# A causal mask as a matrix product, finer waits and finer pacing in a two-branch attention kernel

## The chip, the cores and the metric

The kernel runs on one core of one Trainium2 chip. The metric is the device time of one execution in microseconds (us). One core has five engines that each work through their own instruction list in order: TensorE (PE, matrix products; its weight loads are a row of their own, PEld), VectorE (DVE), ScalarE (ACT), GpSimd (POOL) and SyncE (SP, which issues transfers). Engines wait for one another only through semaphores.

## What is computed

Two attention branches over the same 2048 x 576 input are mixed by a sigmoid gate. Branch A is recurrent: 64 segments of 32 tokens, each with 8 memory tokens that are an output of the segment before.

```python
def _A_ref(x, mem0, Wq, Wk, Wv, Wo, seg_len):
    ...
    mask = (idx[:, None] < M) | (idx[:, None] >= idx[None, :])
    mem = mem0
    for s in range(n_seg):
        xs = x[:, s * seg_len:(s + 1) * seg_len, :].copy()
        h = jnp.concatenate([mem, xs], axis=1)
        ...
        scores = jnp.where(mask[None, None], scores, -1000000000.0)
        p = _softmax(scores, axis=-1)
        o = jnp.einsum('bhqk,bhke->bhqe', p, v)
        o = jnp.einsum('bhte,hed->btd', o, Wo)
        mem = o[:, :M, :].copy()
        outs.append(o[:, M:, :])
    return jnp.concatenate(outs, axis=1)

def _B_ref(x, wqkv, wo):
    ...
    p = _softmax(scores, axis=-1)
    o = jnp.einsum('bhqk,bhkd->bhqd', p, v)
    ...
g = _sigmoid((x * gate_w).sum(-1, keepdims=True))
return g * a + (1 - g) * b
```

Branch A has 32 heads of 128, 40 positions in a segment (8 + 32) and a 40 x 40 softmax, here called the small softmax. Branch B is an ordinary softmax attention with 32 heads of 18 over 2048 x 2048 scores.

## The kernel before

**A planner writes the order.** The program does not issue instructions where the Python code stands. Each piece of work is recorded with `add` (L132): engine or engines that may do it, an estimated duration, the pieces it depends on, a priority, and the buffers ("tokens") that it takes and gives back. `Plan.run` (L151) and `Plan.choose` (L251) then place the pieces on the five engines one after the other, and this fixes the instruction order of every engine. The priorities and thresholds come from the table `RANKS` (L17), one row for each 16 segments. The duration estimates are used for the order alone: on the chip every engine runs its list as fast as the semaphores let it. When the planner foresees a gap on PE of more than about 0.3 us, it puts in a filler (L829): a group of four products with a zero matrix, added to an accumulator that is open anyway (`warm`, L182).

**Branch B** is cut into 512 visits (L842 on). A visit is a group of four score products on PE (`sb`, L858), one exponential of 128 x 2048 on ACT (`etb`, L867), and a group of four value products on PE (`ob`, L876). The scores of a visit fill four of the eight PSUM banks and there is one such buffer, so the next score group waits for the exponential. Every 16 visits an output is normalised by four VectorE operations (L904 to L919) and stored by POOL.

**Branch A, one segment.** `ht` (the 8 memory tokens and 24 of the 32 new ones, transposed) is multiplied into six pieces of Q, K and V (`pvv`, L1201, 30 groups of four products), which are copied out of PSUM (`tm`), and Q and K are transposed by DMA (`tt`, L1293) and put in place by VectorE (`qk`, L1302). The heads come in two halves. For each half: 32 score products (`psh`, L1325) into one PSUM bank; an exponential on ACT (`et`, L1335); a minimum with the constant `cap` on DVE (L1341), which is 3e38 where the mask allows and 0 where it forbids; the row sums as 12 small products (`pss`, L1356); a reciprocal on DVE (L1368); its spread over the rows as 12 products (`prb`, L1382); a multiplication on DVE (L1393); 16 products with V (`pso`, L1404); two copies to `ot` (L1414, recorded through the helper lines L472 on ACT and L474 on DVE). The output product (`out_pieces`, L1099; 128 products on L1109 in eight pieces of 16, four to a half) starts for each half when both copies of that half are there. Then `ob_cast` (L1436) copies the result `acc` to `obf`, `ob_bd` (L1439) reads `acc` again in PSUM and multiplies its last 16 columns with a mask into `bd`, the fold (`pw`, L1461, 12 small products) turns the memory rows round, and L1471 writes them into the `ht` of the next segment. This loop from `ht` to `ht` is serial over 64 segments.

The last 8 tokens of every segment don't feed the memory: their projections are computed outside the loop in `la` units (`last_unit`, L955, lines L946 and L950), two for each of most segments, and their output product is `lo` (L1490), once per four segments.

**What ties the branches.** The gate list at the end (L1657 to L1663) gives a visit a dependency on a piece of branch A: the first `ahead` visits are free, the last `behind` come after, and the others are dealt over the 64 segments. Before, all visits of a segment depend on one piece, the first projection (`seg_gate[s] = uq0`, L1233).

Of the kernel before, what the change touches and what calls it, by code (L numbers as in the profile page):

```python
# [10 lines left out]
BF16 = mybir.dt.bfloat16  # L11
# [7 lines left out]
        "switch": 0.101, "near": 0, "early": 1.104, "wait": 0.393, "Q0": 2.363, "K0": 2.711, "Q1": 4.67,  # L19
        "K1": 3.397, "V0": 5.924, "V1": 5.379, "t0": 0.94, "t1": 0.398, "ph0": 9.657, "ph1": 0.05, "sm0": 1.041,  # L20
        "sm1": 2.745, "bc0": 0.781, "bc1": 0.697, "po0": 0.142, "po1": 0.573, "op0": 3.391, "op1": 0.536,
        "fo": 2.847, "lo0": 7.697, "lo1": 1.76, "la": 2.503, "ob": 1.356, "eQ": 5.996, "eK": 4.139, "eV": 3.462,
        "co": 11.428, "le": 6.917, "xp": 4.684, "mn": 1.531, "ct": 3.999, "fin": 17.485, "la_gate": 1,
        "lo_gate": 1, "ahead": 53, "behind": 12, "tail": 0.25, "qc": 5.203, "gap": 0.082, "cool": 863.098,
        "tp": 0.05, "cp": 0.05,
    },
    {
        "switch": 0.566, "near": 0, "early": 0.879, "wait": 0.574, "Q0": 2.035, "K0": 2.767, "Q1": 5.001,
        "K1": 3.913, "V0": 5.813, "V1": 5.624, "t0": 2.693, "t1": 3.024, "ph0": 10.481, "ph1": 0.05, "sm0": 1.356,
        "sm1": 2.806, "bc0": 0.705, "bc1": 1.374, "po0": 0.16, "po1": 0.85, "op0": 4.548, "op1": 0.05,  # L30
        "fo": 2.442, "lo0": 6.471, "lo1": 1.6, "la": 2.902, "ob": 1.514, "eQ": 4.303, "eK": 1.887, "eV": 2.757,
        "co": 9.646, "le": 7.257, "xp": 4.622, "mn": 1.072, "ct": 2.98, "fin": 18.697, "la_gate": 1, "lo_gate": 1,
        "ahead": 53, "behind": 12, "tail": 0.25, "qc": 4.212, "gap": 0.025, "cool": 604.648, "tp": 0.059,
        "cp": 2.5,
    },
    {
        "switch": 0.933, "near": 0.062, "early": 0.442, "wait": 0.458, "Q0": 3.101, "K0": 3.266, "Q1": 4.507,
        "K1": 3.879, "V0": 5.715, "V1": 5.233, "t0": 1.746, "t1": 1.52, "ph0": 8.719, "ph1": 0.544, "sm0": 0.98,
        "sm1": 2.636, "bc0": 0.878, "bc1": 1.593, "po0": 0.05, "po1": 0.666, "op0": 4.211, "op1": 0.142,
        "fo": 1.753, "lo0": 7.609, "lo1": 3.613, "la": 2.285, "ob": 0.938, "eQ": 3.915, "eK": 1.776, "eV": 4.854,  # L40
        "co": 10.047, "le": 4.881, "xp": 4.775, "mn": 0.059, "ct": 3.249, "fin": 19.989, "la_gate": 1,
        "lo_gate": 1, "ahead": 53, "behind": 12, "tail": 0.399, "qc": 4.172, "gap": 0.021, "cool": 833.588,
        "tp": 1.502, "cp": 2.715,
    },
    {
        "switch": 0.842, "near": 0.056, "early": 0.478, "wait": 0.257, "Q0": 0.05, "K0": 3.207, "Q1": 4.114,
        "K1": 3.963, "V0": 4.848, "V1": 4.944, "t0": 1.753, "t1": 1.675, "ph0": 9.689, "ph1": 0.593, "sm0": 2.541,
        "sm1": 2.776, "bc0": 2.467, "bc1": 1.373, "po0": 2.298, "po1": 0.768, "op0": 7.231, "op1": 0.203,
        "fo": 1.659, "lo0": 7.93, "lo1": 3.297, "la": 0.05, "ob": 1.161, "eQ": 3.254, "eK": 0.05, "eV": 6.854,
        "co": 9.595, "le": 4.095, "xp": 3.302, "mn": 0.33, "ct": 2.917, "fin": 18.443, "la_gate": 1, "lo_gate": 1,  # L50
        "ahead": 53, "behind": 12, "tail": 0.332, "qc": 5.346, "gap": 0.021, "cool": 6051.615, "tp": 2.782,
        "cp": 4.189,
# [23 lines left out]
class Plan:  # L76
# [74 lines left out]
    def run(self):  # L151
# [18 lines left out]
        while len(order) < n + extra:  # L170
# [54 lines left out]
            dirty |= set(free)  # L225
# [7 lines left out]
            for t in op.take:  # L233
                held = self.tokens[t]
                got = max(x for x in held if x[0] <= est + 1e-9)
                held.remove(got)
                op.slots.setdefault(t, []).append(got[1])
                dirty |= set(free)
            for t, taker, k in op.give:
                self.tokens[t].append((op.end + op.tail + self.DRAIN[pick], taker.slots[t][k]))  # L240
                dirty |= set(free)
# [70 lines left out]
def kernel(  # L312
# [68 lines left out]
    cap = const.tile([P, L], BF16, name="cap")  # L381
# [7 lines left out]
    nc.vector.memset(cap[:], 3.0e38)  # L389
# [7 lines left out]
    for jj in range(2):  # L397
        o = 64 * jj
        nc.vector.memset(bsel[o:o + 64, jj:jj + 1], 1.0)
        nc.gpsimd.affine_select(  # L400
            out=cap[o:o + 64, M:L], in_=cap[o:o + 64, M:L], pattern=[[1, seg]],
            compare_op=ALU.is_gt, fill=0.0, base=M + 1, channel_multiplier=-1,
        )
        nc.gpsimd.affine_select(
            out=cap[o:o + 64, 0:M], in_=cap[o:o + 64, 0:M], pattern=[[0, M]],
            compare_op=ALU.is_gt, fill=0.0, base=L, channel_multiplier=-1,
        )
# [59 lines left out]
    LA_COL, PH_COL, SM_COL, BC_COL, FO_COL = False, True, True, True, True  # L467
# [631 lines left out]
    def out_pieces(name, o_of, t0, hf, state, first, last, prio, deps, take):  # L1099
# [18 lines left out]
        for k in range(4):  # L1118
            d = deps if op is None else [op]
# [583 lines left out]
```

## Time and profile before

| | before |
|---|---|
| median of three runs | 1505.62 us (1496.74, 1506.17, 1505.62) |
| the profiled execution, its own time | 1497.41 us |
| its span, first to last instruction | 1495.7 us |
| ACT / DVE / POOL busy, share of the span | 72% / 53% / 37% |
| first fold (end of segment 0) starts at | 183.9 us |
| 63rd and last fold starts at | 1434.0 us |

Between those two folds lie 62 segments, 1250.1 us or 20.2 us each. The first 184 us load weights and make branch B's projections; the last 62 us hold the last segment, the last visits, and the final products and stores.

In the rows of the profile, "x4" counts instructions and a duration ahead of a group of matmuls is the time in which at least one was in the array, so that four products that run side by side in four column strips count once. Ends of matmuls are modelled.

### The profile page before, as it was taken

How to read it: one execution, taken by the hardware profiler on the slowest of the kernel's cores; microseconds unless marked ns; L12 is line 12 of the kernel's file. 1: busy time of each engine (PE TensorE's matmuls, PEld its weight loads, DVE VectorE, ACT ScalarE, POOL GpSimd, SP SyncE). 2: the span in 40 equal slices, each digit the busy share in tenths (PEclk: the TensorE clock that was granted, in tenths of full speed). 3: DMA queues.
4: the chain of work that ended last, by engine and by line, in shares of the span. 5: the costliest groups of instructions: out<-in, count | busy, mean ns of one | idle time of the engine just before them, and what ended most of it. 6: DMA issues, size and time to landing. Idle time of an engine off the chain costs nothing.

```text
span 1495.7 us, 79573 instructions
## 1 busy us (share of the span) xinstructions
PE 1395.7 (93%) x35969; PEld 767.7 (51%) x35969; DVE 799.3 (53%) x1953; ACT 1075.1 (72%) x824; POOL 547.5 (37%) x1182
## 2 busy tenths in 40 slices
PE   7889899999999999999999999999898999989998
PEld 4345555555555544555555545555554544544545
DVE  6344465555555455555555555555555555555565
ACT  2457588887878777777777777777686777767784
POOL 6243145334532355332543325433354333423310
PEclk9899999999999999999999999999999999999999
DMA  6896434233333333433423333433334233432352
GB/s 216 291 302 182 109 79 78 62 67 60 77 57 70 59 76 68 72 62 61 78 66 67 62 63 70 76 61 64 56 81 83 55 56 56 71 52 53 48 147 87
DMA packets 343422, 130.79 MB, mean 87 GB/s; under 512 B 296943, under 2 KB 329159, under 8 KB 343083
## 3 DMA queue, kind: packets, MB, share of 16 engines
q1 hardware_dynamic: 314771, 81.20, 27.6%
q0 software_dynamic: 27088, 43.31, 10.5%
q8 instruction: 281, 4.60, 1.3%
q10 hardware_dynamic: 1224, 1.20, 0.3%
q14 instruction: 58, 0.48, 0.1%
HBM read 52.74 MB, written 30.86 MB: 56 GB/s over the span
## 4 chain that ended last, share of the span: by engine, by line
PE 62%; DMA 14%; ACT 11%; DVE 6%; issue 5%; SPq 1%; ACTq 0%; POOL 0%; DVEq 0%; POOLq 0%
PE pvv L1201 22%; ACT etb L867 10%; PE sb L858 9%; PE ob L876 7%; PE acc L1109 7%; DMA tt<-tm 7%; PE ob L829 3%; PE pv L946 3%; DMA v_sb<-tm 2%; PE pso L1404 2%; PE pq L664 1%; PE psh L1325 1%; DMA qtd<-stg 1%; PE po L1626 1%; PE prb L1382 1%
## 5 line engine op out<-in xcount | busy, mean ns | idle before, releaser
L867 ACT ACTIVATE etb<-sb 128x2048 bf16<-128x2048 f32 x512 | 961.3, 1878 | 344.3 <-PE sb L858 319.1
L474 DVE CAST tm<-pvv 128x512 bf16<-128x512 f32 x330 | 228.0, 691 | 264.5 <-PE pvv L1201 262.0
L1201 PEld LDWEIGHTS <-ht 128*32 128x32 bf16 x7680 | 201.7, 97 | 195.7 <-DVE ht L1471 18.9
L858 PE MATMUL sb<-qch,kch 32*128 32x512 bf16 x2048 | 204.9, 385 | 19.1 <-ACT etb L867 14.2
L876 PE MATMUL ob<-etb,vch 128*32 128x512 bf16 x2048 | 205.1, 390 | 5.4 <-DMA vch<-vgd 2.4
L1109 PE MATMUL acc<-wo,ot 128*32 128x144 bf16 x8192 | 159.5, 228 | 4.2 <-issue 4.0
L1109 PEld LDWEIGHTS <-ot 128*32 128x32 bf16 x8192 | 136.4, 98 | 15.9 <-issue 7.0
L1201 PE MATMUL pvv<-wq_m,ht 128*32 128x512 bf16 x2048 | 136.3, 380 | 2.5 <-DVE ht L1471 1.6
L858 PEld LDWEIGHTS <-kch 32*128 32x128 bf16 x2048 | 62.1, 91 | 148.9 <-issue 126.7
L1201 PE MATMUL pvv<-wv_m,ht 128*32 128x512 bf16 x2048 | 137.6, 379 | 0.0
L1201 PE MATMUL pvv<-wk_m,ht 128*32 128x512 bf16 x2048 | 133.9, 380 | 0.5 <-DVE vl L474 0.5
L1152 POOL COPY ht<-xg 128x96 bf16<-128x96 bf16 x64 | 17.3, 271 | 279.8 <-PE pvv L1201 278.6
L474 DVE CAST ot<-pso 128x320 bf16<-128x320 f32 x174 | 81.4, 484 | 69.6 <-PE pso L1404 68.9
L829 PE MATMUL ob<-unit,nil 128*32 128x512 bf16 x1512 | 115.7, 379 | 0.2 <-issue 0.2
L876 PEld LDWEIGHTS <-vch 128*32 128x32 bf16 x2048 | 54.8, 93 | 116.0 <-issue 110.7
L1302 DVE COPY qk<-tt 128x512 bf16<-128x512 bf16 x256 | 77.0, 309 | 29.5 <-DMA tt<-tm 27.9
L1393 DVE TENSOR_TENSOR et<-et,prb 128x320 bf16<-128x320 bf16 x128 | 61.8, 484 | 45.2 <-PE prb L1382 43.7
L778 POOL DMA_DIRECT2D qch<-qtd x120 | 61.2, 516 | 62.9 <-PE sb L858 56.7
L778 POOL DMA_DIRECT2D otd<-stage x124 | 62.6, 512 | 58.2 <-DVE stage L919 43.7
L1170 POOL COPY qk<-xl 128x256 bf16<-128x256 bf16 x128 | 51.3, 412 | 72.6 <-PE psh L1325 51.4
L778 POOL DMA_DIRECT2D kch<-ktd x112 | 56.4, 510 | 53.3 <-PE sb L858 51.5
L474 DVE CAST vl<-pv 128x512 bf16<-128x512 f32 x87 | 59.2, 685 | 31.0 <-PE pv L946 12.5
(152 smaller groups left out, 1882.9 us busy)
## 6 DMA issues: line engine op xcount, KB each, us to landing
xl<-qkd SPq DMA_DIRECT2D x64, 128.0 KB
v_sb<-tm SPq DMA_DIRECT2D x256, 32.0 KB
qkd<-vl POOLq DMA_DIRECT2D x48, 128.0 KB, 3.0
wo<-in_A_Wo_dram POOLq DMA_DIRECT2D x4, 1152.0 KB, 7.0
vgd<-vt SPq DMA_DIRECT2D x32, 128.0 KB
wv_m<-in_A_Wv_dram POOLq DMA_DIRECT2D x4, 1024.0 KB, 6.6
wq_m<-in_A_Wq_dram POOLq DMA_DIRECT2D x4, 1024.0 KB, 6.9
wk_m<-in_A_Wk_dram POOLq DMA_DIRECT2D x4, 1024.0 KB, 7.9
```

The costliest lines, as they stand in the source:

```text
L474: nc.vector.tensor_copy(out=out_of(), in_=in_of())
L778: dma(out=rows_, in_=pads) if out else dma(out=pads, in_=rows_)
L829: nc.tensor.matmul(box["ob"][32 * j:32 * j + 32, :], lhsT=nil[:, 0:32], rhs=unit[:, :].unsqueeze(1).to_broadcast([P, 4, P]), start=False, ...
L858: nc.tensor.matmul(sb[:, j, :], lhsT=kc[r, o:o + P], rhs=qt_[r, :], start=True, stop=True, tile_position=(32 * j, 0),)
L867: nc.scalar.activation(out=etb[:, :, :], in_=box["sb", gq, kb][:, :, :], func=ACT.Exp, scale=scale_b)
L876: nc.tensor.matmul(ob[32 * j:32 * j + 32, :], lhsT=vc[:, o + 32 * j:o + 32 * j + 32], rhs=etb[:, j, :], start=(kb == 0), stop=(kb == NKB - ...
L946: nc.tensor.matmul(out_, lhsT=lw, rhs=rw, start=(c == 0), stop=(c == NF))
L1109: nc.tensor.matmul(acc[32 * j:32 * j + 32, :], lhsT=o[:, slot, t0:t0 + CT], rhs=wo[:, h, RW * j:RW * j + RW], start=(first and s_ == 0), s ...
L1170: nc.gpsimd.tensor_copy(out=opened["qk"][:, f, :, 0:16 * L].rearrange("p a (h t) -> p a h t", t=L)[:, :, :, CT:L], in_=box["xlt", s][:, :, ...
L1201: nc.tensor.matmul(pv[32 * j:32 * j + 32, :], lhsT=ht[:, cc, :], rhs=rw, start=(c == 0), stop=(c == NF), tile_position=(0, 32 * j), skip_g ...
L1302: eng.tensor_copy(out=opened["qk"][:, hf, a, 0:16 * L].rearrange("p (j i t) -> p j i t", i=4, t=L)[:, :, :, 0:CT], in_=box["tt", s, a, hf] ...
L1393: nc.vector.tensor_tensor(out=et[:, :], in0=et[:, :], in1=box["prb", s, hf][:, :], op=ALU.mult)
```

## The change

Four edits in the kernel, and a new table of priorities.

1. **The mask.** The VectorE minimum is gone. A constant `veil` (0 where allowed, -30000 where forbidden, 128 x 40 with 64 rows in use) replaces `cap`. Four products of the identity with `veil`, spread over 8 heads (320 columns), start the PSUM bank of the scores; the score products add to it. The sums now wait for ACT's exponential directly.
2. **The output product.** Of the four pieces of a half, the first two wait for the first of the two copies and the last two for the second; before, all waited for both.
3. **The tails.** `ob_bd` reads the bf16 copy `obf` in SBUF instead of `acc` in PSUM, and the PSUM bank is given back after `ob_cast` instead of after `ob_bd`.
4. **The pacing.** A visit depends on one of eight pieces of its segment, in turn, instead of on the first one.

```diff
@@ RANKS: four rows of new values; "ahead": 53 -> 48, "behind": 12 -> 4 in all of them @@
@@ Plan.run: which engines' best candidates are looked up again @@
-            dirty |= set(free)
+            if op.dmas:
+                dirty |= set(free)
...
@@ constants @@
-    nc.vector.memset(cap[:], 3.0e38)
+    nc.vector.memset(veil[:], 0.0)
...
+    nc.gpsimd.affine_select(
+        out=veil[0:64, M:L], in_=veil[0:64, M:L], pattern=[[1, seg]],
+        compare_op=ALU.is_gt, fill=-30000.0, base=M + 1, channel_multiplier=-1,
+    )
...
@@ out_pieces @@
-            d = deps if op is None else [op]
+            d = [*(deps if op is None else [op]), *(halves[k // 2] if halves else ())]
...
@@ psh @@
+                for i in range(4):
+                    o = 32 * (i % 2)
+                    nc.tensor.matmul(
+                        ph[32 * i:32 * i + 32, :], lhsT=ident[:, o:o + 32],
+                        rhs=veil[:, :].unsqueeze(1).to_broadcast([P, 8, L]),
+                        start=True, stop=False, tile_position=(0, 32 * i), skip_group_check=True,
+                    )
                 for r in range(8):
...
-                            start=True, stop=True, tile_position=(0, 32 * i), skip_group_check=True,
+                            start=False, stop=True, tile_position=(0, 32 * i), skip_group_check=True,
...
-            p_ = add(f"ph{hf}.{s}", "PE", 0.44, psh, [*turned, pl], prio=RANK[f"ph{hf}"], mode="col" if PH_COL else "half", take=("pb",), use=0.3, pairs=32 if PH_COL else 16)
+            p_ = add(f"ph{hf}.{s}", "PE", 0.57, psh, [*turned, pl], prio=RANK[f"ph{hf}"], mode="col", take=("pb",), use=0.4, pairs=36)
...
-            m_ = add(f"mn{hf}.{s}", "DVE", 0.337, mn, [x_], prio=RANK["mn"])
...
-            s_ = add(f"sm{hf}.{s}", "PE", 0.12 if SM_COL else 0.1, sm, [m_], prio=RANK[f"sm{hf}"],
+            s_ = add(f"sm{hf}.{s}", "PE", 0.12 if SM_COL else 0.1, sm, [x_], prio=RANK[f"sm{hf}"],
...
-                ots[2 * hf:2 * hf + 2] + wo_loads + ([mids[0]] if hf else []), ("pb",) if hf == 0 else (),
+                wo_loads + ([mids[0]] if hf else []), ("pb",) if hf == 0 else (), [[o] for o in ots[2 * hf:2 * hf + 2]],
...
-                in0=st["acc"][:, P:RW].unsqueeze(1).to_broadcast([P, NF, TR]), in1=bmask[:, :, :], op=ALU.mult,
+                in0=box["obf", s][:, P:RW].unsqueeze(1).to_broadcast([P, NF, TR]), in1=bmask[:, :, :], op=ALU.mult,
...
-        c2 = add(f"bd{s}", "DVE", psum_copy(64), ob_bd, [mids[1], c1, prev.get("fold")], prio=0.3, give=(("pb", acc_state["op0"], 0),))
+        c2 = add(f"bd{s}", "DVE", 0.13, ob_bd, [c1, prev.get("fold")], prio=0.25)
...
+        seg_gate[s] = [uq0, uk0, uq1, uv1, cur["psh1"], cur["pso0"], cur["pso1"], cur["out"]]
...
-            s = min(int((i - ahead) / share), n_seg - 1)
-            vi.deps.append(seg_gate[s])
+            k = min(int(8 * (i - ahead) / share), 8 * n_seg - 1)
+            vi.deps.append(seg_gate[k // 8][k % 8])
```

The rebuilt program's instruction lists differ in these counts: PE 512 more mask products (128 groups of four) and 576 fewer fillers (1516 to 940); DVE 128 fewer minimums, 31 more `tm` copies, 16 more `ot` copies, 24 fewer `v_sb` copies; ACT 31 fewer `tm` copies and 16 fewer `ot` copies; POOL 24 more `v_sb` copies. The number of transfers is the same on every queue.

## Prediction

> **What bounds the kernel now.** I read the page's busy shares first, then the stages, then one segment's timeline, then the waits. Busy shares and stages (columns: length, then busy time and count of PE, PEld, DVE, ACT, POOL, then the granted clock, the share of the DMA engines, GB/s):
>
> ```profile
> PE 1395.7 (93%) x35969; PEld 767.7 (51%) x35969; DVE 799.3 (53%) x1953; ACT 1075.1 (72%) x824; POOL 547.5 (37%) x1182
> ```
>
> ```profile
> 184.00:1434.00 1250.00, 1186.65 (x33364) 651.59 (x33360) 677.82 (x1680) 946.35 (x717) 474.91 (x1014) 1.00 0.35 65
> ```
>
> The 62 segments between the first fold and the last one are 84% of the span; PE is busy in 95% of them at full clock. But busy PE is partly fillers. The costliest groups show how much, and the price of a minimum and of an exponential:
>
> ```profile
> L867 ACT ACTIVATE etb<-sb 128x2048 bf16<-128x2048 f32 x512 | 961.3, 1878 | 344.3 <-PE sb L858 319.1
> L829 PE MATMUL ob<-unit,nil 128*32 128x512 bf16 x1512 | 115.7, 379 | 0.2 <-issue 0.2
> L1341 DVE TENSOR_TENSOR et<-et,cap 128x320 bf16<-128x320 bf16 x128 | 43.3, 339 | 12.0 <-ACT et L1335 10.1
> ```
>
> The timeline of a segment's end shows why fillers are there: the serial loop makes PE wait (start, length, what).
>
> ```profile
> 1428.39 0.24 PE L1356 MATMUL pss<-bsel,et 128*32 128x2 bf16 x12
> 1428.48 0.82 PE L829 MATMUL ob<-unit,nil 128*32 128x512 bf16 x12
> ...
> 1430.46 0.37 PE L1404 MATMUL pso<-et,v_sb 64*128 64x40 bf16 x16
> 1430.76 1.86 PE L1109 MATMUL acc<-wo,ot 128*32 128x144 bf16 x106
> 1430.87 0.89 DVE L474 CAST ot<-pso 128x320 bf16<-128x320 f32 x2 [0.76 <-PE pso L1404]
> ```
>
> The reader is to see three filler groups right after the sums, and 22 of the 128 output products missing from the last-but-one row: they wait for both copies. What PE itself waited for, all execution long (total, times, longest):
>
> ```profile
> PE sb L858 <- ACT etb L867: 14.2, 39, 2.0
> PE psh L1325 <- DVE qk L1302: 7.5, 17, 1.6
> PE pso L1404 <- DMA v_sb<-tm: 7.3, 9, 1.8
> PE pss L1356 <- DVE et L1341: 6.9, 14, 1.5
> ```
>
> So PE's own work plus many small waits of the loop set the time; no other engine is full.
>
> **A yardstick for PE.** From the starts of the matmuls in the trace I took, for each kind followed by each kind, the usual time from one start to the next: the median inside a run of one kind, the lower quartile where kinds change. (A group of four 512-column products starts every 0.216 us; a group of four 144-column products every 0.063.) Added along PE's order, this gives the time in which PE would issue everything if it waited for nothing: 1343.4 us before, of 1495.7. The other 152.3 us are waits: 40.7 ahead of the first fold (transfers), 101.6 between the first and last fold (1.6 a segment), 6.3 behind, and 3.7 from the last matmul's start to the end. The program's two PE orders are known, so the same sum can be made for the new one: 1322.2 us, 21.1 less. Its parts follow.
>
> **Fillers.** 378 groups become 235. With the turn to what follows they take 103.0 us before and 62.0 after: -41.0. This is PE time that the planner no longer needs for padding; it is a gain only if the real gap is gone too. That is what the other three edits must do, so I price the loop.
>
> **The mask product.** 128 groups of four 320-column products. No such row exists; the two neighbours are 144 columns at 0.063 us and 512 at 0.216, so 320 lie at 0.063 + 176 x 0.153/368 = 0.136 us. 128 x 0.136 = 17.4, and with the turns 18.4 us, all on the bound engine. It waits only for its PSUM bank, so where PE waits for `qk` anyway (7.5 us in 17 cases) some is hidden: 17 cases x 0.136 = 2.3 at most. I take +18.4 - 1.4 = +17.0.
>
> **The minimum taken away.** 128 x 0.339 = 43.3 us of DVE, which is 53% busy, cost nothing by themselves. On the loop, the time from the end of the exponential to the first sum is 0.79 us in the median, 0.56 at the best tenth, and of that a direct hand-over from ACT needs about 0.1 (the exponential to a following product took 0.05 to 0.2). So the loop loses about 0.7 us for the second half of a segment; the first half's is mostly covered by other products. Who is late next: the reciprocal and the spread, on the same two engines.
>
> **The output product.** The second copy ends 0.28 us after the first (median, second half), and in 37 of 64 segments the products start within 0.15 us of it. The loop gains up to 0.28 us. The first half has cover.
>
> **The tails.** `bd` takes 0.215 us from PSUM (the group of L1439), in series between the output product and the fold. 64 elements from SBUF: the 320-element form takes 0.484 from PSUM (L1393) and 0.325 from SBUF (L1341), 0.16 less, so bounds are 0.06 to 0.215; I take 0.13, a gain of 0.085 a segment. [...] POOL's copy of `ot` (0.41) stands just ahead of `bd`, ending 0.03 us before it at 717 us; the two overlapped in 1 of 64 segments. By the row: -0.085 x 62 = -5.3 us of loop. [...] I take the row. The bank given back 0.2 us earlier helps whoever waits for one of three; no wait in the list names that, so nothing.
>
> **Loop and PE together.** 0.7 + 0.28 + 0.085 = 1.07 us off a loop of 20.2 a segment, 66 us over 62 segments, is the most if the loop alone decided. PE's sum between the folds falls only from 1148.5 to 1136.0, because the mask is added and because 459 visits instead of 451 stand there. I expect neither end: the fillers gone (-41 with turns) are the part of the 1.07 that the planner turned into order.
>
> **Pacing.** The gate and the visit are both on PE, whose order is fixed, so this adds no wait; it only spreads the score groups. Behind each waiting score group stand all later products of branch A. Between the folds, PE's own work from one score group to the next is under 2.43 us, the shortest cycle that score, exponential, score shows (the fifth percentile of start to start), by 41 us in total before and 54 us after, so bunching gets a bit worse, not better: more visits share less work. Before, the score groups' waits came to 21.7 us of those 41 by my sum; in proportion +7 us. Against it, ACT loses 47 copies between exponentials (31 of 0.58, 16 of 0.42, 25 us), and DVE as a net 43.3 - 31 x 0.69 - 16 x 0.48 + 24 x 0.30 = 21 us.
>
> **The other waits.** The sums' wait (8.2 us by my sum, 6.9 in the list) mostly goes: -6. Waits inside and ahead of the output product (8.6) fall by a third: -3. Score products behind `qk` and V products behind the `v_sb` transfer stay; with a shorter loop the transfer could be late more often, +2. Emptier DVE and ACT: -10 of the remaining 50. Sum with bunching: -10.
>
> **Clock.** Fewer fillers mean less activity. [...] Between the folds the longest stretch without a product was 1.8 us, the granted clock 1.00, and the longest filler run that can fall idle is eight groups, 1.9 us. By the row: 0. [...] I take 0.
>
> **Ends.** Ahead of the first fold transfers decide; PE's sum falls 2.4 there, and I give none of it (+2). Behind the last fold PE's sum falls 6.2, as 11 visits are left instead of 18, but the order there ends with the last value groups, then all of `lo` (32 groups, 2.1 us), then the store, reload and gating of that result (8.6 us from 1481.8 to 1490.4), where before `lo` lay inside the last visit: +5.
>
> **Sum.** Fillers -41.0, mask +17.0, other order +1.5, waits -10, ends +7: -25.5 on 1495.7, a span of 1470. The own time lies 1.7 above the span, 1472; the median of the runs shown lies 8 us above the profiled execution, since two of three do; the new one's runs may lie at either level, so I say 1474.
>
> **Rivals.**
> (B) The loop decides nearly alone, and PE's padding was covering it: 66 us less between the folds, +6 at the ends, 1436 us, 1440 as a median. For it: fillers stand wherever the loop is open. Against it: PE's sum leaves 1136 there, and visits need 459 x 2.43 = 1115, so 1184 would be nearly without waits.
> (C) The order's gain is given back: if PE's waits grow with the shortness of the gaps as they did before (I sorted gaps by length and gave each the mean wait of its class), the new order waits 130 us instead of 101.6, +28, and -21 + 28 + 7 gives 1510 as a span; with half of that 1496, 1500 as a median. This is also the case that the change does nothing measurable.
> (D) Slower: score and exponential become the bound. Place: the score buffer. Price: the whole 54 us of shortfall on top of the other waits instead of among them, -21 + 54 = +33, 1529, 1532 as a median. It decides once the score groups' waits exceed about 45 us. Against it: 7.4 visits a segment x 2.43 = 18.0 us still fit into 19.8.
>
> **How the numbers follow.** Likeliest 0.55 (own range 1458 to 1490), B 0.15, C 0.20, D 0.10. About 1% is what a measurement can tell from no change here: the three runs shown lie 0.6% apart. Faster by over 1% is below 1490.6: nearly all of the first (0.53) and B, 0.68. Within 1%: C and 0.02, 0.22. Slower: 0.10. The range leaves out D and the far half of B: 1440 to 1505.
>
> **What would show it.** Right: 2.2 fillers a segment fewer and segments of about 19.8 us; a mask group at 0.13 to 0.14 us; sums at about 0.1 us behind the exponential; `bd` near 0.13; the wait of score groups for exponentials under 25 us. Wrong: that wait over 40 us (D), segments at 20.2 with new PE gaps where fillers stood (C), segments under 19.2 (B), or a granted clock under 0.97 between the folds.

## The result and the profile after

| | before | after |
|---|---|---|
| median of four runs | 1505.73 us (1496.74 to 1506.17) | 1484.38 us (1478.91 to 1488.50) |
| ratio | | 0.9871, 95% interval 0.9825 to 0.9918 |
| profiled execution, own time; span | 1497.41; 1495.7 | 1480.68; 1478.9 |
| first fold starts at | 183.9 | 178.6 |
| last fold starts at | 1434.0 | 1422.5 |

The kernel became faster by 1.3%, about 20 us. 1474 was forecast, 31.6 us under the 1505.6 then known; the medians lie 21.4 apart, two thirds of that. The same views as before follow. The busy shares, the stage between the folds, and the costliest groups:

```profile
PE 1376.1 (93%) x35897; PEld 771.8 (52%) x35905; DVE 779.7 (53%) x1840; ACT 1060.4 (72%) x785; POOL 563.5 (38%) x1204
```

```profile
181.00:1434.00 1253.00, 1184.54 (x33560) 661.58 (x33556) 668.21 (x1589) 949.62 (x686) 498.11 (x1051) 1.00 0.35 66
```

```profile
L869 ACT ACTIVATE etb<-sb 128x2048 bf16<-128x2048 f32 x512 | 961.5, 1878 | 313.2 <-PE sb L860 290.0
...
L1111 PE MATMUL acc<-wo,ot 128*32 128x144 bf16 x8192 | 168.8, 227 | 12.0 <-issue 11.2
...
L831 PE MATMUL ob<-unit,nil 128*32 128x512 bf16 x940 | 77.7, 379 | 2.8 <-issue 2.8
```

PE is as full as before (93%) and 20 us shorter; the filler row (L831) lost 38 us of busy time. So this picture says only that PE is still the bound. The two operations that had no row before, the mask product and the new form of `bd`, each from the view of its tile (count, then shortest, median and longest in ns, first and last start; the count at the end of a row is of a sample):

```profile
L1318 PE MATMUL psh<-veil,ident x512: 296/299/310, 167.9 to 1439.1; 128*32 128x320 bf16 x171
```

```profile
L1433 DVE TENSOR_TENSOR bd<-obf,bmask x64: 191/192/337, 178.6 to 1447.6; 128x64 bf16<-128x64 bf16 x64
```

The 299 ns are one product's own time, from its start to its modelled end. What PE pays is the time from one group of four to the next kind, and that is 0.125 us from the start of its last product and 0.136 from that of its first (medians of 128 groups). `bd` takes 0.192 us; it took 0.215. PE's waits in the whole execution (total, times, longest):

```profile
PE sb L860 <- ACT etb L869: 20.1, 51, 2.0
PE acc L1111 <- issue: 16.6, 28, 1.2
PE psh L1326 <- DVE qk L1303: 7.4, 14, 1.4
...
PE pso L1398 <- DMA v_sb<-tm: 3.0, 5, 1.7
```

Two changes are to be seen. The sums' wait for the minimum (6.9 us before) is gone. And a row that was small before, the output product that waits for "issue" (6.2 us in 12 cases), is now 16.6 us in 28. "Issue" means that the profile shows nothing that the product waited for. The end of the last segment but one shows this wait in place:

```profile
1417.32 0.24 PE L1350 MATMUL pss<-bsel,et 128*32 128x2 bf16 x12
1417.41 0.60 PE L831 MATMUL ob<-unit,nil 128*32 128x512 bf16 x8
...
1419.31 0.37 PE L1398 MATMUL pso<-et,v_sb 64*128 64x40 bf16 x16
...
1419.70 0.89 DVE L476 CAST ot<-pso 128x320 bf16<-128x320 f32 x2 [0.45 <-PE pso L1398]
...
1419.83 1.11 PE L1111 MATMUL acc<-wo,ot 128*32 128x144 bf16 x60
...
1421.29 0.75 PE L1111 MATMUL acc<-wo,ot 128*32 128x144 bf16 x36 [0.35 <-issue]
```

Two filler groups stand behind the sums instead of three. The first 32 of the 60 products belong to the first half, so the second half begins at about 1420.35, ahead of the second copy's end at 1420.59: the finer wait works. But after 28 products of the second half PE stops. The second copy is needed only from the 33rd on, and it ended 0.7 us before PE goes on. This stop is the main surprise of this case; the last part shows what ends it.

**Where the 16.8 us of span came from.** By the prediction's yardstick, between the folds: 1250.1 us became 1243.9, PE's own sum 1148.5 became 1136.0, the waits 101.6 became 107.9. Ahead of the first fold 5.4 us were gained, but the first fold of this same kernel, profiled a second time, lay at 183.8, so this part is not the change's. Behind the last fold the time to the last product's start fell from 57.8 to 50.8 (51.0 in the second profile), and 1.9 us of it went to the stretch behind.

### The profile page after: what moved, and what is told of

Read it like the earlier page. It is cut to its first block, busy times and chain, and to the rows that moved or that the text cites. A ratio compares the mean times of both kernels' runs of the same rounds, so it can differ in the third digit from the quotient of the medians.

```text
span 1478.9 us, 79421 instructions
## 1 busy us (share of the span) xinstructions
PE 1376.1 (93%) x35897; PEld 771.8 (52%) x35905; DVE 779.7 (53%) x1840; ACT 1060.4 (72%) x785; POOL 563.5 (38%) x1204
## 4 chain that ended last, share of the span: by engine, by line
PE 65%; ACT 14%; DMA 11%; DVE 5%; issue 4%; SPq 1%; POOL 0%; ACTq 0%; DVEq 0%; POOLq 0%
PE pvv L1203 24%; ACT etb L869 13%; PE sb L860 10%; PE acc L1111 8%; PE ob L878 7%; DMA tt<-tm 6%; PE pv L948 4%; PE pq L666 2%; PE pso L1398 2%; PE ob L831 2%; PE pv L952 1%; PE po L1621 1%; PE prb L1376 1%; DMA v_sb<-tm 1%; PE psh L1326 1%
## 5 line engine op out<-in xcount | busy, mean ns | idle before, releaser
L476 DVE CAST tm<-pvv 128x512 bf16<-128x512 f32 x361 | 249.2, 691 | 269.1 <-PE pvv L1203 262.8
L860 PE MATMUL sb<-qch,kch 32*128 32x512 bf16 x2048 | 203.6, 385 | 27.3 <-ACT etb L869 20.1
L878 PE MATMUL ob<-etb,vch 128*32 128x512 bf16 x2048 | 201.5, 386 | 0.7 <-ACT etb L869 0.6
L1111 PE MATMUL acc<-wo,ot 128*32 128x144 bf16 x8192 | 168.8, 227 | 12.0 <-issue 11.2
L860 PEld LDWEIGHTS <-kch 32*128 32x128 bf16 x2048 | 65.1, 91 | 153.7 <-issue 132.0
L1203 PE MATMUL pvv<-wk_m,ht 128*32 128x512 bf16 x2048 | 138.4, 379 | 0.0
L476 DVE CAST ot<-pso 128x320 bf16<-128x320 f32 x190 | 87.5, 484 | 81.6 <-PE pso L1398 79.7
L1242 POOL COPY v_sb<-tm 32x512 bf16<-32x512 bf16 x78 | 48.2, 618 | 190.2 <-DVE tm L476 120.2
L1387 DVE TENSOR_TENSOR et<-et,prb 128x320 bf16<-128x320 bf16 x128 | 61.9, 486 | 43.3 <-PE prb L1376 40.7
L831 PE MATMUL ob<-unit,nil 128*32 128x512 bf16 x940 | 77.7, 379 | 2.8 <-issue 2.8
```

What stands on the lines that cost most here:

```text
L476: nc.vector.tensor_copy(out=out_of(), in_=in_of())
L831: nc.tensor.matmul(box["ob"][32 * j:32 * j + 32, :], lhsT=nil[:, 0:32], rhs=unit[:, :].unsqueeze(1).to_broadcast([P, 4, P]), start=False, ...
L860: nc.tensor.matmul(sb[:, j, :], lhsT=kc[r, o:o + P], rhs=qt_[r, :], start=True, stop=True, tile_position=(32 * j, 0),)
L878: nc.tensor.matmul(ob[32 * j:32 * j + 32, :], lhsT=vc[:, o + 32 * j:o + 32 * j + 32], rhs=etb[:, j, :], start=(kb == 0), stop=(kb == NKB - ...
L1111: nc.tensor.matmul(acc[32 * j:32 * j + 32, :], lhsT=o[:, slot, t0:t0 + CT], rhs=wo[:, h, RW * j:RW * j + RW], start=(first and s_ == 0), s ...
L1203: nc.tensor.matmul(pv[32 * j:32 * j + 32, :], lhsT=ht[:, cc, :], rhs=rw, start=(c == 0), stop=(c == NF), tile_position=(0, 32 * j), skip_g ...
```

## The experiments

Two theories are set against each other throughout. A: the time follows PE's own sum, so each part of the change is worth its difference in that sum. B: the serial loop decides, so each part is worth what it takes out of the loop. A third one in an expectation, also where it is lettered C, belongs to that experiment alone and is not the prediction's rival C. The kernel before had medians of 1498.54 us on the chip of experiments 1 to 4, 1504.51 on that of 5 to 8, and 1503.94 and 1503.63 on that of 9 to 12, so kernels are compared by their ratio to it on the same chip; the changed kernel's was 0.987 twice, with intervals of about 0.004 to either side. Its "level" on a chip is 0.987 times the kernel before there, good to some 5 us. In experiment 5 the medians alone give 0.990, so differences to that run are up to 5 us smaller than the ratios make them. "Planned anew" means that the planner made another order for the kernel; where "same order" is said, every engine keeps the changed kernel's order.

**1. The minimum back on VectorE, planned anew.**

```diff
-                for i in range(4):
-                    nc.tensor.matmul(ph[32 * i:32 * i + 32, :], lhsT=ident[:, o:o + 32], rhs=veil...)
...
-                            start=False, stop=True, tile_position=(0, 32 * i), skip_group_check=True,
+                            start=True, stop=True, tile_position=(0, 32 * i), skip_group_check=True,
...
+            m_ = add(f"mn{hf}.{s}", "DVE", 0.337, mn, [x_], prio=RANK["mn"])
...
-            s_ = add(f"sm{hf}.{s}", ..., sm, [x_], ...)
+            s_ = add(f"sm{hf}.{s}", ..., sm, [m_], ...)
```

> The changed kernel with the mask alone undone: the minimum on VectorE is back on the loop, the mask products are gone; the planner orders it anew with the new table. Theory A (time is PE's own sum plus waits of about the size of now): PE's sum by the yardstick is 1325.4 us, 3 more than in the changed kernel (18 less of mask, 19 more of fillers), so 1487, within noise of the changed kernel, with 72 more filler groups. Theory B (the loop decides): 0.7 us back on the loop in 62 segments, +43, 1527. Theory C (mask products on a full PE are a loss): 17 us faster than the changed kernel, 1467.

Measured: 1509.25 us (1508.11 to 1516.94) against 1498.54; ratio 1.0082 (1.0053 to 1.0112). That is 30 us above the changed kernel's level on this chip (0.987 x 1498.54 = 1479). PE's sum is only 3 us larger; the waits between the folds are 132.9 instead of 107.9. A falls for this part; B is right in direction, too large in size. Not all of it is the minimum: a good half of the new waits are late packets of instructions (table behind experiment 12).

**2. Finer waits and SBUF tails undone, planned anew.**

```diff
-                wo_loads + ..., ("pb",) if hf == 0 else (), [[o] for o in ots[2 * hf:2 * hf + 2]],
+                ots[2 * hf:2 * hf + 2] + wo_loads + ..., ("pb",) if hf == 0 else (),
-                in0=box["obf", s][:, P:RW]...
+                in0=st["acc"][:, P:RW]...
```

> The changed kernel with the finer waits of the output product and the tails from SBUF both undone, mask and pacing kept. Theory A: PE's sum is 1337.6, 15.4 more than in the changed kernel (52 more filler groups), so 1500, the larger half of the gain. Theory B: 0.28 + 0.085 us back on the loop in 62 segments, +23, 1507. Theory C' (both edits have cover): 1484, as the changed kernel.

Measured: 1507.32 us (1504.17 to 1509.06); ratio 1.0056 (1.0035 to 1.0077), 28 us above the changed kernel's level. PE's sum is 15.4 larger (287 filler groups instead of 235) and the waits 11.0. Here the planner answered a longer loop with more fillers, so most of the loss does appear in the sum; the table behind experiment 12 shows late packets here too. The run takes away two parts at once; experiments 9 and 11 part them.

**3. One gate for all visits of a segment, planned anew.**

```diff
-            vi.deps.append(seg_gate[k // 8][k % 8])
+            vi.deps.append(seg_gate[k // 8][0])
```

> The changed kernel with all visits of a segment gated by its first projection, as before; the rest kept. Theory A: PE's sum is 1326.6, 4.4 more (18 more filler groups), so 1489. Rival (pacing is what gains): back to 1500 or more, with score groups waiting over 45 us for exponentials. Rival (pacing bunches score groups worse): faster than the changed kernel, 1475, with waits of score groups under 25 us.

Measured: 1487.17 us (1486.84 to 1492.61); ratio 0.9933 (0.9910 to 0.9955). By the ratio 8 us above the changed kernel's level; but between the folds its trace has 1244.8 us, no more than the changed kernel's 1243.9 and 1245.6. The pacing's worth stays between nothing and 8 us.

**4. The kernel before with the new table alone.**

```diff
@@ RANKS: the four new rows in place of the old ones; nothing else @@
```

> The kernel before with nothing but the new table of priorities (48 visits ahead, 4 behind). Theory A: PE's sum is 1343.8 as before (1343.4), so 1505 less about 7 at the tail with 11 visits instead of 18, 1498. Rival (the table alone does it, the four edits are decoration): 1484 as the changed kernel.

Measured: 1516.78 us (1513.84 to 1521.04); ratio 1.0131 (1.0108 to 1.0155): slower than before by 18 to 20 us. That the table alone makes the time falls: it is worth nothing without the edits.

**5. The changed kernel again**, on the chip of experiments 6 to 8.

> The changed kernel once more, as the measure for the three runs beside it: 0.987 of the kernel before. All theories alike.

Measured: 1489.29 us (1487.16 to 1492.08) against 1504.51; ratio 0.9870 (0.9839 to 0.9901).

**6. The minimum on VectorE, same order.** The mask groups are left out, and the minimum stands right behind its exponential.

```diff
-                for i in range(4):
-                    nc.tensor.matmul(ph[32 * i:32 * i + 32, :], lhsT=ident[:, o:o + 32], rhs=veil...)
...
+                nc.vector.tensor_tensor(
+                    out=e3, in0=e3, in1=veil[:, :].unsqueeze(1).to_broadcast([P, 8, L]), op=ALU.min
+                )
```

> The changed kernel's own order on PE, kept product by product; only the 128 mask groups are left out and the minimum stands on VectorE right behind its exponential instead. This separates the price of the minimum from a new order. Theory A (PE's own sum): 18 less, 17 to 18 us faster than the changed kernel. Theory B (the loop): 0.7 us more on the loop's second half in 62 segments, +43, less 17 of mask, so 26 slower, the sums waiting for the minimum for over 30 us in all. Both halves on the loop: +60.

Measured: 1507.26 us (1504.94 to 1515.34); ratio 1.0020 (0.9990 to 1.0051), 18 us above experiment 5. PE's sum is 17.9 less, the waits between the folds 144.0 instead of 109.6. Its waits:

```profile
PE acc L1112 <- issue: 22.6, 29, 1.3
PE sb L861 <- ACT etb L870: 22.3, 56, 2.0
PE pss L1348 <- DVE et L1332: 10.7, 35, 0.7
```

The third row is back, larger than before the change; this order was planned without the minimum. With the order held, putting the minimum back costs about 35 us of waits (18 + 17), and the mask costs 17 on PE: the exchange is worth 18 here by the medians. By the yardstick 21.3 of the 34.4 us of new waits stand ahead of the sums, and 8.3 are longer stops for issue. These 8.3 are not the minimum's own: the kernel has 1024 instructions fewer on PE, so the places of the others in PE's list have moved, and experiment 8 shows what that alone can cost. Without them the exchange is worth about 10.

**7. The fillers left out, same order.**

```diff
-    plan.warm = {"col": warm_col, "full": warm_full}
+    plan.warm = {"col": lambda e: None, "full": lambda e: None}
```

> The changed kernel's order with its 235 filler groups not issued (they add zero; the result is the same). PE's sum is 33 us less. If each filler stands in a gap of the loop that is there anyway: the time of the changed kernel within 5 us, the granted clock between the folds 0.98 or more. If fillers stand in the way: up to 33 us faster. [...]

Measured: 1496.67 us (1490.78 to 1500.91); ratio 0.9925 (0.9889 to 0.9960), 7 us above experiment 5. The stage from 180 to 1430 us in experiment 5 and here:

```profile
180.00:1430.00 1250.00, 1178.98 (x33486) 658.50 (x33484) 664.79 (x1580) 945.18 (x683) 496.57 (x1047) 1.00 0.35 66
```

```profile
180.00:1430.00 1250.00, 1142.34 (x32369) 649.47 (x32369) 658.74 (x1562) 937.62 (x677) 492.37 (x1038) 0.99 0.35 65
```

Between the folds 27.0 us of PE's own sum are gone, and the waits grow by 38.6. Removing the fillers that are left gained nothing, which fits fillers that stand in real gaps. It is not proof: this run also moves the list (8 us more of late packets) and has more half clock (below, up to 12 us by the estimate there). Less these two, the waits grew by some 19 us for the 27 taken away, so part of the fillers may stand in PE's way. Fillers are a symptom of the loop, and to count them as a gain is right only when the loop is shortened too.

**8. 64 small products ahead of everything, same order.** With their loads they move every later instruction of PE by 128 places in its list. They stand in the start, where PE waited 40.7 us for transfers in the kernel before (the prediction's yardstick).

```diff
+    def pad(e):
+        for _ in range(64):
+            nc.tensor.matmul(pz[:, :], lhsT=nil[:, :], rhs=unit[:, 0:8], start=True, stop=True)
```

> The changed kernel's order unchanged, with 64 small products ahead of everything while PE waits for its first input (their result isn't used). After the change 47 stalls between the folds (32 us in all) stand at PE instructions whose place in PE's list is 192 modulo 256, and the profile's instruction queue moves packets of 16384 bytes. If these are waits for the next packet of instructions, the stalls keep that place in the list and so hit other products, 64 products earlier; their sum can change, since the planner assumed the old places: 20 to 60 us, and the time moves by that, -12 to +28. If they are waits of the output product for its copies, the same products stall again, at 64 modulo 256, and the time doesn't change.

Measured: 1505.10 us (1499.70 to 1507.83); ratio 0.9990 (0.9962 to 1.0017), 16 us above experiment 5. The first fold is not later (182.0 against 183.8); the loss is between the folds, 1269.3 us against 1245.6, and it is one row:

```profile
PE acc L1118 <- issue: 29.3, 40, 1.3
PE sb L867 <- ACT etb L876: 20.5, 50, 2.0
```

In experiment 5 the first row had 17.2 us in 25 cases, the second 19.7 in 47. The order is the same, the score groups' wait is within 1 us, and the half clock between the folds is 6.8 us instead of 3.4; what differs by design is the place in the list. One segment's end:

```profile
1408.37 0.56 PE L1118 MATMUL acc<-wo,ot 128*32 128x144 bf16 x23 [0.52 <-issue]
1408.86 0.37 PE L1405 MATMUL pso<-et,v_sb 64*128 64x40 bf16 x16
1409.16 0.68 PE L1118 MATMUL acc<-wo,ot 128*32 128x144 bf16 x32
1409.77 0.39 PE L867 MATMUL sb<-qch,kch 32*128 32x512 bf16 x4
1410.10 1.05 PE L1118 MATMUL acc<-wo,ot 128*32 128x144 bf16 x53
1412.39 0.37 PE L1118 MATMUL acc<-wo,ot 128*32 128x144 bf16 x11 [1.24 <-issue]
```

From one stop to the next PE issued 23 + 16 + 32 + 4 + 53 = 128 products, each with its weight load: 256 instructions. The last part tells what has this size.

**9. `bd` from PSUM, same order.**

```diff
-                in0=box["obf", s][:, P:RW]...
+                in0=st["acc"][:, P:RW]...
```

> The changed kernel with every engine's order kept and one operand changed back: the tails are multiplied out of the accumulator in PSUM instead of the copy in SBUF. After the change the multiplication takes 0.192 us against 0.215, and the step from the last output product to the written memory rows 1.35 us against 1.30, so the trace gives this edit no gain. If that is right: the time of the changed kernel within 4 us. By the prediction's step (0.085 us of loop in 62 segments): 5 us slower than it. [...]

Measured: 1486.97 us (1482.16 to 1490.58) against 1503.94; ratio 0.9888 (0.9864 to 0.9912). Not to be told from the changed kernel.

**10. The planner counts PE's instructions with a correction, planned anew.** The planner in both kernels charges PE when 128 products come within 3.6 us of the 128 before. Its count leaves out some instructions; here it was corrected.

```diff
-        self.count += n
+        self.count += n * self.DRIFT
```

> The changed kernel with one thing more in the planner: it counts the extra instructions on PE (0.12% of all, waits that are instructions of their own), so that the places where it expects a new packet of instructions don't drift away from the real ones by 36 products over the program. PE's sum by the yardstick is 1321.3, as now (1322.2). If late packets are what the new order loses most by, a planner that knows their place avoids more of the dense ones: stalls at 192 modulo 256 under 25 us instead of 30 to 32, and 1477 to 1485 where the changed kernel has 1487. If a stall is the same wherever it stands, no change.

Measured: 1553.42 us (1537.62 to 1562.02); ratio 1.0308 (1.0268 to 1.0349). A clear miss: 70 us above what was expected. The late packets did not go under 25 us; they are 42.2 in the trace of its slowest run (1562.02). Between the folds that trace has 1299.6 us, and the waits that grew most stand ahead of the score products of the small softmax (32.4 us against 13.9 in the changed kernel) and of the V products; 27 us ran at half clock. Why this order is so much worse, though PE's sum is 1321.3, is open.

**11. Each half waits for both copies, same order.** The first product of each copy's eight heads change places, so the half starts only when both copies are there.

```diff
-                for s_ in range(lo, lo + 4):
+                for n_ in range(lo, lo + 4):
+                    s_ = {0: 8, 8: 0}.get(n_, n_) if halves else n_
```

> The changed kernel with its own order of work on every engine; only in each half of the output product the first product of the first copy's 8 heads and the first of the second copy's change places, so that the half again starts when both copies are there. In the changed kernel's trace the second half starts ahead of the second copy's end in 22 of 64 segments (by 0.34 us), the first half in 12. If the finer wait is worth what it lets PE do early: 22 x 0.34 = 7 us slower at most, 1492 to 1496 where the changed kernel stands at 1487 to 1489. If the products that start early only come to wait elsewhere (for the second copy's heads, for a packet of instructions): within 3 us of the changed kernel.

Measured: 1495.05 us (1489.73 to 1501.67) against 1503.63; ratio 0.9948 (0.9929 to 0.9968), 11 us above the changed kernel's level; between the folds 1252.9 us, 7 to 9 above its two traces.

```profile
PE acc L1112 <- issue: 14.9, 22, 1.7
PE acc L1112 <- DVE ot L476: 7.0, 18, 0.7
```

The second row is new, and its 7.0 us agree in size with the 22 x 0.34 = 7 that the second half's early starts were worth. With the order and the list held, the finer wait is a gain of 7 to 11 us.

**12. A new order and nothing else.**

```diff
-    SWITCH = 0.1
+    SWITCH = 0.101
```

> All edits and the table kept; only the planner's estimate of PE's turn between two kinds of products goes from 0.100 to 0.101 us, which is used for the order alone. The order of PE is the same up to product 9184 of 35,900 and another one behind it; the yardstick gives 1321.2 us for it against 1322.2, with as many fillers (235) and visits between the folds (459). If the kernels that were planned anew with one part undone lost time because of the part: this one stays within 4 us of the changed kernel, 1484 to 1492. If a table fits only the order that it was searched for, and any other order loses: 1497 to 1510, and then the losses of those kernels say little of their parts.

Measured: 1490.51 us (1483.57 to 1492.70); ratio 0.9908 (0.9884 to 0.9933), 6 us above the changed kernel's level by the ratio, 2 to 4 between the folds. This new order cost a few us, not 28. Experiment 10 shows that an order can also fall out much worse, so one such run does not prove that the 28 to 30 us of experiments 1 and 2 are those of the parts taken away.

**Late packets in all these kernels.** In every trace the stops pile up at one place modulo 256 of PE's list, of which the last part tells more. Their sum (stops of over 0.1 us, against each kernel's own usual steps), and the time between the folds with and without it, in us:

| | between the folds | late packets | the rest |
|---|---|---|---|
| before | 1250.1 | 22.1 | 1228.0 |
| changed | 1243.9 | 32.8 | 1211.1 |
| changed, experiment 5 | 1245.6 | 31.1 | 1214.5 |
| 1, minimum back | 1272.5 | 47.6 | 1224.9 |
| 2, waits and tails undone | 1270.4 | 44.7 | 1225.7 |
| 3, one gate | 1244.8 | 23.8 | 1221.0 |
| 4, table alone | 1274.9 | 32.3 | 1242.6 |
| 6, minimum, same order | 1262.7 | 38.3 | 1224.4 |
| 7, no fillers | 1257.2 | 39.2 | 1218.0 |
| 8, list moved | 1269.3 | 52.9 | 1216.4 |
| 9, tails, same order | 1247.8 | 34.3 | 1213.5 |
| 11, both copies | 1252.9 | 30.6 | 1222.3 |
| 12, new order | 1248.0 | 34.7 | 1213.3 |

The last column is an estimate, since a stop may hide a wait that would have come anyway, and each row is one trace. By it the change took about 15 us off the work and waits between the folds, and 9 to 11 of them went to later packets. Experiment 8 comes back to the changed kernel's level, as a shift of the list should. The minimum is worth 10 to 14 whether planned anew or not, the finer waits 8 to 15, and the pacing, which the times could not show, 7 to 10, hidden in experiment 3 by 8 us fewer late packets.

## Why the prediction was right, and which terms were off

The direction was right, and so was the first half of the mechanism: the sums' wait goes, and 143 filler groups that covered the loop go with it. The likeliest case's own range, 1458 to 1490, holds the 1484. That the number came so near is in part luck: of the 25.5 us forecast for the span 16.8 came, 17.7 less than forecast between the folds and 8.9 more at the ends, of which the 5.4 ahead of the first fold are not the change's. The term that was put at nothing without a reason is the instruction stream: the part on the kernel says that every engine runs its list as fast as the semaphores let it, and PE's late packets took 22 us between the folds before and 31 to 33 after.

**The waits, forecast -10, measured +6.3.** By kind, in us between the folds ("score groups" has 24.6 here where the prediction counted 21.7 by a narrower sum, and "sums" 9.3 instead of 8.2):

| | before | after | forecast | measured |
|---|---|---|---|---|
| score groups | 24.6 | 34.3 | +7 | +9.7 |
| sums | 9.3 | 2.6 | -6 | -6.7 |
| output product | 8.6 | 21.7 | -3 | +13.1 |
| V products | 18.7 | 7.4 | +2 | -11.3 |
| all others | 40.4 | 41.9 | -10 | +1.5 |

The growth of the score groups' waits and the fall of the sums' came in about the size forecast; that bunching is what made the first was not tested apart. Two steps failed. "Waits inside and ahead of the output product fall by a third": they grew to two and a half times, and 15.3 of the 21.7 us are late instruction packets. "Emptier DVE and ACT: -10 of the remaining 50": this was a guess without a row behind it; the other waits grew by 1.5. That the V products' wait fell by 11.3, where +2 was forecast, is not explained by any experiment here.

The totals of the yardstick depend on how the steps are sorted. With one table of usual steps from all these traces, PE's sum between the folds falls by 19 us instead of 12.5 and the waits grow by 13 instead of 6.3; each of the four named rows keeps its direction.

**The loop, forecast 0.7 + 0.28 + 0.085 us a segment at most.** Exponential to sums fell from 0.79 to 0.35 us in the median, from 0.41 to 0.05 in the best twentieth: the mechanism is as stated, 0.44 instead of 0.7. That PE is often still at other work would fit, and is not shown. The finer wait lets the second half start 0.34 us ahead of the second copy's end in 22 of 64 segments; experiment 11 puts it at 7 to 11 us, 0.11 to 0.18 a segment, under the 0.28 given as the most.

**The tails, forecast 0.085, measured 0.023 for `bd` and nothing for the loop.** The estimate took the saving of a 320-column form for a 64-column one. From the last output product to the memory rows being written the median went from 1.30 to 1.35 us: the fold starts sooner after `obf` (0.11 instead of 0.19), but its last products still wait for `bd`. Experiment 9 finds no gain. `bd` is 191 to 193 ns in 61 of 64 cases, inside the row's bounds of 0.06 to 0.215 us and above the 0.13 taken. Of the three longer ones (255, 334 and 337 ns), those of 255 and 337 overlap a POOL copy of `otl`; two others that overlap one took 191 and 193.

**The mask** came as interpolated: 0.136 forecast, 0.125 to 0.136 measured.

**The ends, forecast -0.4 and -1.2, measured -5.4 and -5.1.** The first is the spread of the start: 178.6 to 187.3 in the profiles of kernels with this order. The second is the term "+5" that was set against a sum 6.2 smaller: `lo` and the store at the end took back 1.1 of it, not 5.

**The clock, forecast 0, was right for this kernel** (1.00 between the folds, rounded; one stretch of 3.4 us at half clock). The prediction read over the three such stretches of the trace before, at 649, 834 and 1178 us, each behind 3.4 us that were not idle (PE busy for 1.90, 1.88 and 2.68 us). The last part has more of them.

**The rivals of the prediction.** B fell: nothing near 66 us came off the time between the folds. C had the sign of the waits right (they grew as the gaps got shorter), but by 6.3 us, or 13 by the other sorting, and not by the 28 of its full price. D fell: the score groups' wait by the list is 20.1, under the mark of 25. Experiments 1 and 6 show that theory A, on which the sum rests, is not enough either: PE's own sum told nothing of what the minimum costs. It came near here, as planner and edits moved the sum and the loop together.

**What the parts are worth in the new order**, from the experiments: mask by product 18 (order held) to 30 us (planned anew), finer waits 7 to 11 (order held; 28 together with the tails, planned anew), pacing 0 to 8, tails nothing. Less the late packets, these are 10 to 14, 8 to 15 and 7 to 10. They add up to more than the 20 us gained, and the table without the edits cost 20 in the old kernel; so the parts cannot be added over two different orders, and how much of the table's cost remains in the changed kernel was not tried.

## What to carry to other kernels

Where a planner pads gaps of a serial loop, price an edit by the loop's step that it removes and look at the padding only as the measure of the gap: taking the padding alone away gained nothing, and putting the removed step back cost 18 us where PE's sum alone promised a gain of 18. When a stretch of small products on PE shows waits for "issue", count products from one stop to the next; if it comes to 128 with their loads, look whether each stop ends at the same distance behind a packet of the instruction queue. Here the 42 longest of the changed kernel did, 1.15 to 1.8 us behind one, and shifting the list by 128 places changed the time by a per cent (16 us). Take these stops out before two orders are compared. A forecast of remaining waits should name a row for each, since the one lump without a row was the one that failed.

## What the runs showed of the hardware

**PE's instructions come in packets, and a packet can be late.** The queues' part of the page (packets, MB, share of the DMA engines), for the changed kernel and for the one without fillers:

```profile
q8 instruction: 281, 4.60, 1.4%
```

```profile
q8 instruction: 273, 4.47, 1.3%
```

4.60 MB in 281 packets are 16,384 bytes each. 940 fillers fewer are, with their loads, 1880 instructions fewer, and 8 packets go; without the mask products it is 1024 fewer, and 4 packets go (277). Both fit 256 instructions a packet: 1880 / 256 = 7.3, 1024 / 256 = 4. So does the whole: 35,905 products and as many loads (experiment 5, also 281 packets) are 280.5 times 256. The stops between the folds pile up at one place modulo 256 of PE's list: 50 of them with 32.8 us in the changed kernel, 36 with 22.1 us before, 70 with 52.9 us in experiment 8. In experiment 8 it is the same place as in experiment 5, though every product has moved by 128 instructions. Sorted by the time since the last such place (five kernels together), the mean stop is 0.69 us at 2.5 to 3 us, 0.22 at 3 to 3.5, 0.04 at 3.5 to 4, and 0.01 beyond; between the folds no two packets landed closer than 3.28 us in the changed kernel (median 4.16) and 3.15 before. 128 output products with their loads issue in 2.0 us (64 in a row take 1.00 in the median), so a run of them outpaces the packets; a mean packet of this kernel lasts 1478.9 / 281 = 5.3 us, which would do. The stops go with the time since the last such place, not with the mean rate, and they took 22 to 53 us between the folds. That moving the list costs 16 us is shown by experiment 8. That the stops are waits for packets is shown by the transfers themselves, which the trace has one by one: all 42 stops of over 0.25 us in the changed kernel and all 61 in experiment 8 end 1.15 to 1.8 us after a packet has landed, and of 261 passings of that place none in the changed kernel and one in experiment 8 come sooner. Where PE did not stop, most passings (176 of 209 in the changed kernel) come later than that. A transfer took 0.88 to 1.74 us in the changed kernel, 1.15 in the median. What asks for a packet, and when, no record here tells.

**PE's clock was halved after stretches that were not idle.** Three stretches of the kernel without fillers (length, PE's busy time, granted clock, share of the DMA engines, GB/s):

```profile
1133.90:1137.30 3.40, 1.28 (x52) 0.99 0.42 70
1137.30:1144.10 6.80, 5.79 (x180) 0.50 0.54 76
1144.10:1147.50 3.40, 2.79 (x108) 1.00 0.08 24
```

The 3.4 us ahead of the half clock had PE busy for 1.28 us. In the changed kernel the one such stretch (1120.3 to 1123.7) follows 3.4 us with 2.29 us busy. In the kernel before, the three had 1.90, 1.88 and 2.68 us busy ahead of them. None of these five was idle. Each of the four in the kernel before and the changed one lasted 3.41 us. Without fillers there were 27 us at half clock between the folds instead of 3.4; if PE were the bound in all of them, that is 23.6 / 2 = 12 us by estimate, more than the 7 that experiment 7 lost in all. The kernel before, with 378 filler groups, had three such stretches and the changed one, with 235, had one, so the number of fillers alone does not set it. What else brings a half clock about was not measured.
